# Attention by pairs of heads: two 64-column V products and four 32-column sums side by side in TensorE's array

## The chip, the cores and the metric

One core of one Trainium2 chip. The metric is the device time of one execution in microseconds (us). Engines: PE is TensorE, DVE is VectorE, ACT is ScalarE, POOL is GpSimd, and SP issues DMAs.

## The reference, cut to what matters

```python
def _attn_ref(q, k, v):                          # 4 batches, 8 heads, 576 positions, 64 wide
    scores = scale * np.matmul(q, k.transpose(0, 1, 3, 2))
    scores = np.where(block_i >= block_j, scores, -1e9)      # blocks of 64 positions
    scores = scores - np.max(scores, axis=-1, keepdims=True)
    attn = np.exp(scores)
    attn = attn / (np.sum(attn, axis=-1, keepdims=True) + 1e-09)
    return np.matmul(attn, v)

x = _moe_ref(x=attention_as_(2304, 512), ...)    # h = x @ w_in; (h * cos(h)) @ w_out
return _moe2_ref(x=x, ...)                       # 8 experts, weighted by a normalised gate
```

The change is in the attention alone, which stands first in the program.

## The kernel before

All on-chip tensors lie with the contracted index on partitions. `attention()` takes the 32 heads one after another, in an order written out by hand (the program order of each engine is the order of the calls). For head i the calls are:

- `load`, `high_both`, `high_parts`, `low_parts`, `move_k_lo`, `move_q_hi`: q and k of a later head are fetched and each split into a rounded high part and the rest (F32R operands `QA`, `KA`, `QB`, `KB`, two buffers each), by ACT, POOL, DVE and DMAs.
- `peak(i, 0)`, `peak(i, 1)`: six rough score products into PSUM tile `px`. `find` takes row maxima on DVE into `nm`, `turn` transposes them on PE, `maxima` puts them into rows of `QA` on DVE, so that the score product subtracts them.
- `weights(i, part)`, four parts: score products (12 F32R matmuls) into one-bank PSUM tiles `sp`, `sq`, `sr`, `sc`, each turned into weights by one exp on ACT (`ep`, `eq`, `er`, `ec`).
- `pv(i, c)`, c from 0 to 4: seven F32 matmuls with the weights as moving and a block of V as stationary operand into PSUM tile `o`. V of an even head has a 65th column of ones, V of an odd head is 128 wide (ones in column 0, V in 64 to 127), so that the sum of the weights comes out in one more partition of `o`.
- `evac(i)`: ACT copies `o` and the sums to SBUF. `sums`, `fetch`, `invert`, `give`, `spread` carry the sums of a pair of heads through DRAM, invert them and spread them over partitions; `scale` multiplies on DVE, `x_hi` and `x_lo` split the result into `xh`, `xl`.
- `some`, `conv.load`: steps of an unrelated conversion of weights, spread over the heads.

Behind the attention the feed-forward part begins with `h` products on the first rows of `xh`. An F32 matmul of the program appears in the trace as two instructions (x2), an F32R one as one.

Of the kernel before, what the change touches and what calls it, by code (L numbers as in the profile page):

```python
# [45 lines left out]
def attention_moe_kernel(ctx: ExitStack, tc: tile.TileContext, qk, v, w_a, gate, w_b, out):  # L46
# [11 lines left out]
    eps = top.tile([128, 80], F32, name="eps")[:, 0:2]  # L58
    nc.vector.memset(eps, 0.0)
    nc.vector.memset(eps[D:D + 1, 0:1], EPS)  # L60
    nc.vector.memset(eps[0:1, 1:2], EPS)
# [92 lines left out]
    def attention():  # L154
        with tc.tile_pool(name="at1", bufs=1) as p1, tc.tile_pool(name="at2", bufs=2) as p2, \
# [3 lines left out]
            KP = S + D  # L159

# [4 lines left out]
            KAP, KBP = (p1.tile([128, 2 * KP], F32R, name=n) for n in ("ka", "kb"))  # L165
            KA, KB = ([t[:, j * KP:j * KP + S] for j in range(2)] for t in (KAP, KBP))
            QB = [p1.tile([128, S], F32R, name=f"qb{j}") for j in range(2)]
            HI = p1.tile([128, S], F32R, name="hi")
# [8 lines left out]
            odd_sums = (post.tile([128, S], F32, tag="lt", name="rawl", bufs=1), tt[0])  # L177
# [5 lines left out]
            st, EP, EQ, ER, EC, SUMS, SR, INV, ps_t, ps_o = ({} for _ in range(10))  # L183
# [5 lines left out]
            def load(i):  # L189
                st[i] = p2.tile([128, S], F32, tag="st", name="st")  # L190
                nc.sync.dma_start(out=st[i][0:64, :], in_=qk[i][0:64, 1, :])
                nc.sync.dma_start(out=st[i][64:128, :], in_=qk[i][64:128, 0, :])

            def load_v(i):
                b, h = divmod(i, H)
                vt, c = V[i % 2], VC[i % 2]
# [18 lines left out]
            def pad():  # L215
                nc.gpsimd.memset(quarter, 0.25)
                ka, kb = (t.bitcast(F32).rearrange("p (j n) -> p j n", n=KP)[:, :, S:] for t in (KAP, KBP))
                nc.gpsimd.memset(kb, 0.0)
                nc.gpsimd.memset(ka[0:96], 0.0)
                nc.gpsimd.memset(ka[96:102], MASK)  # L220
                nc.gpsimd.memset(ka[96:101], -1.0)

            def zeros(j):
                nc.gpsimd.memset(QA[j][:, 0:64].bitcast(F32), 0.0)
                nc.gpsimd.memset(KA[j][64:128, :].bitcast(F32), 0.0)

            def minus(j):
                nc.gpsimd.memset(KA[j][96:101, :].bitcast(F32), -1.0)
                nc.gpsimd.memset(QA[j][96:102, 384:640].bitcast(F32), 1.0)
                nc.gpsimd.memset(NM[j], 0.0)  # L230

            def mask_q(j, copy):
                copy(QA[j][64:96, 64:640], diag[64:96, 64:640], None)

            def mask_k(j, copy):
                for h in range(2):
                    out = KA[j][64:72, 64:576].rearrange("p (t h n) -> p t h n", h=2, n=64)[:, :, h, :]
                    copy(out, step(1 - h), MASK)

            def by_dve(out, in_, factor):  # L240
                if factor is None:
                    nc.vector.tensor_copy(out=out, in_=in_)
                else:
                    nc.vector.tensor_scalar(out=out, in0=in_, scalar1=factor, scalar2=None, op0=ALU.mult)

            def by_act(out, in_, factor):
                nc.scalar.activation(out, in_, AF.Copy, scale=1.0 if factor is None else factor)
# [5 lines left out]
            def ones_of_v():  # L253
                nc.gpsimd.memset(V[0][:, :, D:D + 1], 1.0)
                nc.gpsimd.memset(V[1][:, :, 0:D], 0.0)
                nc.gpsimd.memset(V[1][:, :, 0:1], 1.0)

            def high_both(i):
# [1693 lines left out]
```

## Time and profile before

| | |
|---|---|
| median of 3 runs | 2051.07 us (2050.14 to 2052.83) |
| profiled execution, own time | 2051.26 us |
| its span in the trace | 2049.2 us |
| PE busy | 2038.3 us, 99% of the span |
| DVE, ACT, POOL busy | 77%, 52%, 36% |
| granted TensorE clock | 1.00, that is 2.4 GHz |
| attention on PE | from the start to 189.28 us |

Busy time of PE says that it always had a matmul in flight, not how full the array was. Starts of matmuls follow each other by the columns that they stream; their printed durations hold the way through the array too.

### The profile page before, as it was taken

The numbers are of one execution on the slowest core, as the hardware profiler recorded it, in microseconds if no ns is written. First come the engines' busy times: TensorE is split into PE (matmuls) and PEld (weight loads), VectorE is DVE, ScalarE is ACT, GpSimd is POOL, SyncE is SP. The second block draws the span as 40 slices with busy tenths as digits, with TensorE's granted clock in tenths as the row PEclk, the third lists the DMA queues.
The fourth block names the chain that finished last, engine by engine and source line by source line (L and its number), as shares of the span: only waits on it lengthen the run. The fifth ranks groups of instructions, "written<-read, shape, count | busy, mean of one in ns | idle before, by whom it ended". The sixth has DMA issues, their size and how long they took to land.

```text
span 2049.2 us, 34723 instructions
## 1 busy us (share of the span) xinstructions
PE 2038.3 (99%) x12549; PEld 1921.3 (94%) x12549; DVE 1577.4 (77%) x2801; ACT 1059.0 (52%) x1873; POOL 735.6 (36%) x569
## 2 busy tenths in 40 slices
PE   9999999999999999999999999999999999999999
PEld 7888999899989998989899999999999999999998
DVE  7887897876778788887776777777777777777776
ACT  7887775554464433334333444544455444445443
POOL 4553330000015444454541333344444333333332
PEclk9999999999999999999999999999999999999999
DMA  6666775574454577766666555555555655555552
GB/s 168 187 185 183 258 264 188 209 265 165 144 190 170 200 247 240 278 217 211 223 240 208 200 173 203 180 180 188 191 198 183 210 178 197 176 203 181 185 184 103
DMA packets 202714, 407.48 MB, mean 199 GB/s; under 512 B 44944, under 2 KB 90512, under 8 KB 202544
## 3 DMA queue, kind: packets, MB, share of 16 engines
q1 hardware_dynamic: 202544, 405.28, 58.6%
q8 instruction: 99, 1.62, 0.3%
q14 instruction: 71, 0.58, 0.1%
HBM read 289.48 MB, written 106.58 MB: 193 GB/s over the span
## 4 chain that ended last, share of the span: by engine, by line
PE 93%; DVE 3%; ACT 2%; DMA 1%; issue 0%; POOL 0%; ACTq 0%; SPq 0%; DVEq 0%
PE acc L846 8%; PE p L526 8%; PE p L525 7%; PE p L524 7%; PE hx L524 6%; PE hx L525 6%; PE hx L526 6%; PE acc L526 4%; PE acc L525 4%; PE acc L524 4%; PE o L360 4%; PE hy L525 3%; PE hy L524 3%; PE hy L526 3%; PE h L524 2%; PE h L526 2%
## 5 line engine op out<-in xcount | busy, mean ns | idle before, releaser
L1552 POOL TENSOR_TENSOR w<-s,w 128x512 fp32r<-128x512 f32 x148 | 232.8, 1573 | 403.1 <-ACT w L1551 382.4
L1648 DVE SCALAR_TENSOR_TENSOR oa<-p,P,oa 128x256 f32<-128x256 f32 x627 | 271.9, 477 | 69.3 <-PE p L526 67.5
L526 PE MATMUL p<-w,xl 128*128 128x256 f32 x870 | 245.1, 282 | 0.0
L525 PE MATMUL p<-w,xh 128*128 128x256 f32 x810 | 227.9, 281 | 0.0
L524 PE MATMUL p<-w,xh 128*128 128x256 f32 x810 | 227.4, 281 | 0.0
L666 POOL TENSOR_TENSOR wv<-stg,wv 128x512 fp32r<-128x512 f32 x62 | 110.9, 1807 | 226.9 <-ACT wv L662 215.3
L1552 POOL TENSOR_TENSOR w<-raw,w 128x512 fp32r<-128x512 f32 x73 | 115.1, 1577 | 186.2 <-ACT w L1551 180.4
L526 PEld LDWEIGHTS p<-w,xl 128*128 128x128 f32 x870 | 164.6, 189 | 0.1
L525 PEld LDWEIGHTS p<-w,xh 128*128 128x128 f32 x810 | 153.1, 189 | 0.0
L524 PEld LDWEIGHTS p<-w,xh 128*128 128x128 f32 x810 | 152.7, 189 | 0.0
L526 PE MATMUL acc<-wv,hs 128*128 128x512 f32 x384 | 150.8, 393 | 0.0
L525 PE MATMUL acc<-wv,hs 128*128 128x512 f32 x384 | 150.6, 392 | 0.0
L524 PE MATMUL acc<-wv,hs 128*128 128x512 f32 x384 | 150.0, 391 | 0.0
L629 POOL TENSOR_TENSOR s<-stg 128x256 f32<-128x256 f32 x60 | 47.2, 808 | 286.4 <-PE acc L846 282.3
L525 PE MATMUL p<-w,xl 128*128 128x256 f32 x492 | 138.2, 281 | 0.0
L524 PE MATMUL p<-w,xl 128*128 128x256 f32 x492 | 138.0, 280 | 0.0
L1493 DVE SCALAR_TENSOR_TENSOR oa<-acc,P,oa 128x512 f32<-128x512 f32 x168 | 123.8, 744 | 11.6 <-PE acc L526 10.8
L524 PE MATMUL hx<-th,w 128*128 128x384 f32 x384 | 129.4, 337 | 0.7 <-ACT c L1736 0.7
L525 PE MATMUL hx<-tl,w 128*128 128x384 f32 x384 | 128.8, 336 | 0.0
L526 PE MATMUL hx<-th,w 128*128 128x384 f32 x384 | 128.6, 335 | 0.0
L1590 ACT ACTIVATE xh<-raw 128x768 fp32r<-128x768 f32 x138 | 114.8, 840 | 14.5 <-DVE raw L1608 7.7
L526 PE MATMUL p<-w,xh 128*128 128x256 f32 x432 | 121.8, 282 | 0.6 <-DVE xh L1598 0.6
(388 smaller groups left out, 6351.3 us busy)
## 6 DMA issues: line engine op xcount, KB each, us to landing
w<-w1d SPq DMA_DIRECT2D x128, 512.0 KB
w<-w1d SPq DMA_DIRECT2D x128, 384.0 KB
stg<-in_w_b_dram SPq DMA_DIRECT2D x64, 512.0 KB
s<-td SPq DMA_DIRECT2D x83, 256.0 KB
s<-in_w_b_dram SPq DMA_DIRECT2D x65, 256.0 KB
wo<-wvd SPq DMA_DIRECT2D x32, 512.0 KB
w1d<-wah SPq DMA_DIRECT2D x32, 512.0 KB
w1d<-wal SPq DMA_DIRECT2D x32, 512.0 KB
```

The costliest lines, as they stand in the source:

```text
L360: nc.tensor.matmul(o[:, q0:q1], vt[:, c], e, start=c == 0, stop=True, skip_group_check=c > 0)
L524: nc.tensor.matmul(ps, lh, rh, start=first, stop=False, skip_group_check=go_on)
L525: nc.tensor.matmul(ps, lh, rl, start=False, stop=False, skip_group_check=go_on)
L526: nc.tensor.matmul(ps, ll, rh, start=False, stop=last, skip_group_check=go_on)
L629: eng.tensor_tensor(out=out, in0=in0, in1=in1, op=op)
L666: eng.tensor_tensor(out=t[:, DM:2 * DM], in0=src, in1=t[:, 0:DM].bitcast(F32), op=ALU.subtract)
L846: nc.tensor.matmul(acc[half, b][:, at:at + w_], w[:, s], h[:, t0:t0 + w_], start=f == 0 and i == 0 and at == 0, stop=f == F1 - 1 and i == ...
L1493: nc.vector.scalar_tensor_tensor(out=o, in0=acc, scalar=p, in1=o, op0=ALU.mult, op1=ALU.add)
L1552: nc.gpsimd.tensor_tensor(out=t[:, DM:2 * DM], in0=raw, in1=t[:, 0:DM].bitcast(F32), op=ALU.subtract)
L1590: nc.scalar.activation(self.h[o], self.get(o), func)
L1648: nc.vector.scalar_tensor_tensor(out=o, in0=ps, scalar=p, in1=o, op0=ALU.mult, op1=ALU.add)
```

## The change

Heads are taken in pairs p = (a, b). The V products of the two heads go into two halves of the array's columns (stationary operand 64 columns wide, output partitions 0 to 63 and 64 to 127 of the one PSUM tile `o`), alternating head by head. V has no column of ones; `pe_sums(p)` makes the sums by 20 matmuls of their own per pair with 32 columns of ones as stationary operand, in four column tiles (head h, column group t). `weights` has two parts with two-bank PSUM tiles `spq`, `src` and one exp each (832 and 768 columns). `evac` is two ACT instructions per pair. `QA`, `KA`, `QB`, `KB` have four buffers each. `scale` runs on POOL in the loop. `peak(.., "o")` and `turn(.., o)` use `o` as scratch between two pairs. The start brings four heads in before the first V products; `direct` splits q and k of heads 0 to 3 by ACT and POOL without DMAs.

```diff
-            V = [p1.tile([128, 336], F32, name="v0")[:, 0:5 * (D + 1)].rearrange("p (c n) -> p c n", n=D + 1), p1.tile([128, 5, 2 * D], F32, name="v1")]
-            VC = [slice(0, D), slice(D, 2 * D)]
+            V = [p1.tile([128, 5, 2 * D], F32, name=f"v{j}") for j in range(2)]
+            E = [[p1.tile([128, n], F32, name=f"e{n}") for n in (832, 768)],
+                 [far(n, F32, "e") for n in (832, 768)]]
...
+            o = pso.tile([128, 1024], F32, name="o")
...
+            def direct(i):
+
+                nc.scalar.activation(KB[i][64:128, 0:S], st[i][0:64, :], AF.Copy)
+                nc.scalar.activation(QB[i][0:64, :], st[i][64:128, :], AF.Copy)
+                for t, r in ((KB, slice(0, 64)), (QB, slice(64, 128))):
+                    nc.gpsimd.tensor_tensor(out=t[i][r, 0:S], in0=st[i][r, :], in1=HI[i % 2][r, :].bitcast(F32),
+                                            op=ALU.subtract)
...
+            def peak(i, u, tag):
...
+                ps = psx.tile([128, 1024], F32, tag="x", name="px") if tag == "x" else o
...
+            def turn(i, ps):
+                ps_t[i] = ps[0:101, 832:960]
+                nc.tensor.transpose(ps_t[i], NM[i % 2], ident)
...
-            def weights(i, part):
...
+            def weights(i, part, then=None):
+
+                at0, blocks = ((0, ((3, 320, 256, 256), (0, 256, 320, 0), (4, 320, 256, 576), (0, 0, 256, 512))),
+                               (64, ((1, 128, 448, 64), (2, 256, 320, 512))))[part]
+                ps = pst.tile([128, 1024], F32, tag=("pq", "rc")[part], name=("spq", "src")[part])
...
+                if then:
+                    then(ps)
+                e = E[i % 2][part]
+                nc.scalar.activation(e, ps[:, at0:at0 + (832, 768)[part]], AF.Exp, scale=0.125)
+                return ps
...
-            def pv(i, c):
-                m = D + 1 if i % 2 == 0 else 2 * D
...
+            def pv(p):
+                for c, q0, q1, part, at in ((0, 0, 256, 0, EQ), (0, 256, 576, 0, EP), (1, 128, 256, 1, ER),
+                                            (1, 256, 576, 1, ER + 128), (2, 256, 576, 1, EC),
+                                            (3, 384, 576, 0, EP + 320), (4, 512, 576, 0, EQ + 256)):
+                    for h in range(2):
+                        r = slice(h * D, (h + 1) * D)
+                        nc.tensor.matmul(o[r, 256 + q0:256 + q1], V[p % 2][:, c, r], E[h][part][:, at:at + q1 - q0],
+                                         start=c == 0, stop=True, skip_group_check=True)
+
+            def pe_sums(p):
+                for t, col, n, part, at, new in ((0, 0, 256, 0, EQ, True), (1, 832, 192, 0, EP + 128, True),
+                                                 (0, 832, 128, 0, EP, True), (1, 832, 192, 0, EP + 320, False),
+                                                 (0, 0 + 128, 128, 1, ER, False), (1, 960, 64, 0, EQ + 256, False),
+                                                 (0, 832, 128, 1, ER + 128, False), (1, 832, 192, 1, ER + 256, False),
+                                                 (0, 832, 128, 1, EC, False), (1, 832, 192, 1, EC + 128, False)):
+                    for h in range(2):
+                        r = slice(h * D + 32 * t, h * D + 32 * t + 32)
+                        nc.tensor.matmul(o[r, col:col + n], ones[:, 0:32], E[h][part][:, at:at + n],
+                                         start=new, stop=True, skip_group_check=True)
+
+            def evac(p):
+                nc.scalar.activation(RAW[p % 3], o[:, 256:832], AF.Copy)
+                nc.scalar.activation(sums_of[p % 2].rearrange("p (b n) -> p b n", n=256),
+                                     o.rearrange("p (b n) -> p b n", n=256)[:, 0::3], AF.Identity, bias=eps)
...
+            def scale(p, eng=nc.gpsimd):
+                eng.tensor_tensor(out=XF, in0=RAW[p % 3], in1=RB, op=ALU.mult)
...
+            edges(3)
+            direct(2)
+            high_both(3)
+            q_high(3)
+            k_high(3, KA)
+            px = peak(2, 0, "x")
...
+            sp = weights(1, 0)
...
+            sr = weights(1, 1)
+            direct(3)
+            px = peak(3, 0, "x")
+            turn(2, sp)
+            maxima(2)
+            find(*px)
+            pv(0)
...
+            pe_sums(0)
+            for p in range(1, NP):
...
+                    maxima(b)
...
+                evac(p - 1)
...
+                    if nxt:
+                        find(*peak(a1, 0, "x"))
+                    weights(a, 0)
+                    if nxt:
+                        f = peak(a1, 1, "o")
+                    weights(a, 1)
+                    if nxt:
+                        find(*f)
...
+                fetch(p - 1)
+                if nxt:
+                    f = peak(b1, 0, "x")
+                    weights(b, 0, lambda ps: turn(a1, o))
+                    find(*f)
+                    maxima(a1)
+                else:
+                    weights(b, 0)
+                sr = weights(b, 1)
+                if nxt:
+                    f = peak(b1, 1, "x")
+                pv(p)
+                if nxt:
+                    find(*f)
+                if p > 1:
...
+                    for i in (a2, b2):
+                        high_both(i)
+                        q_high(i)
+                        k_high(i, KA)
+                    for i in (a2, b2):
+                        low_parts(i)
+                        move_k_lo(i)
+                if p > 1:
+                    scale(p - 2)
+                invert(p - 1)
+                give(p - 1)
...
+                some(2 if p % 2 == 0 else 3)
...
+                pe_sums(p)
...
+                    turn(b1, sr)
```

PE, products of an even head with V before, from the middle of the attention (`o` is the output tile, `v_109` V with its ones, `px` and `pt` the rough scores and the transpose):

```order
L360 MATMUL o_1055<-ep_1034,v0_109 65x320
L360 MATMUL o_1055<-eq_1041,v0_109 65x256
L293 MATMUL px_1058<-ka_101,qa1_100 128x448
L293 MATMUL px_1058<-ka_101,qa1_100 128x320
L360 MATMUL o_1055<-er_1046,v0_109 65x128
L360 MATMUL o_1055<-er_1046,v0_109 65x320
L360 MATMUL o_1055<-ec_1051,v0_109 65x320
L320 MATMUL pt_1077<-ident_61,nm1_107 101x128
L360 MATMUL o_1055<-ep_1034,v0_109 65x192
L360 MATMUL o_1055<-eq_1041,v0_109 65x64
```

The same place after: the end of `pv` and the start of `pe_sums` of a pair (`e832`, `e768` are the weights of the first head, `e_122`, `e_123` those of the second):

```order
L357 MATMUL o_131<-e768_121,v1_119 64x320
L357 MATMUL o_131<-e_123,v1_119 64x320
L357 MATMUL o_131<-e832_120,v1_119 64x192
L357 MATMUL o_131<-e_122,v1_119 64x192
L357 MATMUL o_131<-e832_120,v1_119 64x64
L357 MATMUL o_131<-e_122,v1_119 64x64
L368 MATMUL o_131<-e832_120,ones_66 32x256
L368 MATMUL o_131<-e_122,ones_66 32x256
L368 MATMUL o_131<-e832_120,ones_66 32x192
L368 MATMUL o_131<-e_122,ones_66 32x192
```

The seven products of 65 or 128 output partitions per head have become fourteen of 64 per pair, and products of 32 output partitions with the tile of ones stand behind them; the rough scores no longer stand between them.

POOL, the start of the program before (the splits of head 0, then constants, then the first cast for head 1):

```order
L221 MEMSET ka_101 5x2x64
L254 MEMSET v0_109 128x5
L255 MEMSET v1_110 128x5x64
L256 MEMSET v1_110 128x5
L228 MEMSET ka_101 5x576
L229 MEMSET qa1_100 6x256
L230 MEMSET nm1_107 128x101
L263 CAST ka_101<-st_130 64x576
```

POOL, the start after, from the cast for head 2 to that for head 3:

```order
L268 CAST ka_107<-tla_127 64x576
L287 TENSOR_TENSOR kb1_102<-st_145,hi_114 64x576
L287 TENSOR_TENSOR qb1_104<-st_145,hi_114 64x576
L239 MEMSET qa_106 64x64
L240 MEMSET qa_106 6x256
L241 MEMSET ka_108 64x64
L242 MEMSET kb_110 128x64
L287 TENSOR_TENSOR kb_109<-tla_127,hi_113 64x576
L287 TENSOR_TENSOR qb_111<-tla_127,hi_113 64x576
L268 CAST ka_108<-tla_127 64x576
```

Four more subtractions (`TENSOR_TENSOR`, those of `direct(1)` and `direct(2)`) and four constants stand ahead of the cast `ka` for head 3, on which the first rough scores of head 3 wait; on PE these stand ahead of `pv(0)`.

## Rows read from the trace of the kernel before

**Rows 1.** The page: busy time, and the chain that ended last by engine.

```profile
PE 2038.3 (99%) x12549; PEld 1921.3 (94%) x12549; DVE 1577.4 (77%) x2801; ACT 1059.0 (52%) x1873; POOL 735.6 (36%) x569
...
PE 93%; DVE 3%; ACT 2%; DMA 1%; issue 0%; POOL 0%; ACTq 0%; SPq 0%; DVEq 0%
```

**Rows 2.** By stretch: us, then PE, PEld, DVE, ACT, POOL busy, clock, DMA share, GB/s.

```profile
100.12:111.30 11.18, 11.18 (x70) 9.28 (x68) 8.44 (x17) 9.28 (x17) 5.46 (x6) 1.00 0.69 192
16.00:189.28 173.28, 172.97 (x1017) 143.19 (x1017) 139.88 (x263) 141.08 (x260) 83.69 (x82) 1.00 0.65 175
```

**Rows 3.** Timeline of PE: start, us, engine, line, instruction; one pair of heads.

```profile
100.12 0.75 PE L293 MATMUL px<-ka,qa 68*128 68x256 f32 x4
100.71 0.28 PE L332 MATMUL sp<-qb,kb 128*128 128x256 f32 x1
...
102.45 0.70 PE L360 MATMUL o<-ep,v 128*65 128x320 f32 x2
102.99 0.59 PE L360 MATMUL o<-eq,v 128*65 128x256 f32 x2
...
104.54 0.70 PE L360 MATMUL o<-ec,v 128*65 128x320 f32 x2
105.08 0.34 PE L320 MATMUL pt<-ident,nm 128*101 128x128 f32 x1
105.25 0.49 PE L360 MATMUL o<-ep,v 128*65 128x192 f32 x2
...
111.30 0.75 PE L293 MATMUL px<-ka,qa 68*128 68x256 f32 x4
```

**Rows 4.** Groups by form, 16 to 190 us: weight loads of two widths (busy us, mean ns).

```profile
L360 PEld LDWEIGHTS o<-eq,v 128*128 128x128 f32 x64 | 11.7, 189 | 2.6
...
L360 PEld LDWEIGHTS o<-eq,v 128*65 128x65 f32 x60 | 8.2, 137 | 4.8
```

**Rows 5.** Timeline of PE around a gate product of 16 output partitions.

```profile
368.33 0.51 PE L846 MATMUL acc<-gh,wo 128*128 128x512 f32 x2
368.68 0.34 PE L559 MATMUL plt<-xh,ghl 128*16 128x384 f32 x1
...
369.90 0.34 PE L560 MATMUL plt<-xl,gz 128*16 128x384 f32 x1
370.07 0.51 PE L846 MATMUL acc<-gh,wo 128*128 128x256 f32 x2
```

**Rows 6.** Groups by form, 16 to 190 us: ACT and POOL (busy us, mean ns).

```profile
L404 POOL TENSOR_TENSOR xl<-tt,xh 128x576 fp32r<-128x576 f32 x13 | 18.3, 1406 | 6.1 <-ACT xh L400 6.1
L346 ACT ACTIVATE ep<-sp 128x512 f32<-128x512 f32 x31 | 18.1, 585 | 7.8 <-PE sp L333 7.8
...
L346 ACT ACTIVATE ec<-sc 128x320 f32<-128x320 f32 x31 | 13.1, 421 | 0.0
...
L369 ACT ACTIVATE tla<-o 64x576 f32<-64x576 f32 x16 | 10.3, 646 | 11.9 <-PE o L360 8.7 <-ACT hi L259 2.1 <-issue 1.1
...
L370 ACT ACTIVATE rawl<-o,eps 1x576 f32<-1x576 f32 x8 | 5.9, 733 | 0.1
```

**Rows 7.** Timeline of DVE in the same pair of heads.

```profile
101.50 1.15 DVE L315 TENSOR_REDUCE nm<-px 128x1 f32<-128x192 f32 x3
...
105.45 0.83 DVE L324 TENSOR_TENSOR qa<-pt,diag 5x640 fp32r<-5x640 f32 x1 [0.45 <-PE pt L320]
```

**Rows 8.** Timeline of POOL at the start of the program.

```profile
6.50 1.40 POOL L284 TENSOR_TENSOR qb<-st,hi 64x576 fp32r<-64x576 f32 x1
...
10.05 0.31 POOL L229 MEMSET qa<- 6x256 f32 x1
...
10.67 0.66 POOL L263 CAST ka<-st 64x576 fp32r<-64x576 f32 x1
```

**Rows 9.** Timeline of PE at the end of the attention.

```profile
184.84 0.39 PE L333 MATMUL sp<-qa,ka 101*128 101x256 f32 x1 [0.31 <-DVE qa L324]
...
189.28 0.42 PE L524 MATMUL h<-xh 128*128 128x384 f32 x1
```

More of the change, by code (lines that the diff above doesn't have):

```diff
@@ L57, in attention_moe_kernel @@
     nc.vector.memset(half_pi, float(np.pi / 2))
[L58 to L61, printed above, removed]
+    eps = top.tile([128, 80], F32, name="eps")[:, 0:1]
+    nc.vector.memset(eps, EPS)
     xh = top.tile([128, NC, N], F32R, name="xh")
@@ L215, in pad @@
             def pad():
[L216 to L225, printed above, removed]
@@ L240, in by_dve @@
[L240 to L247, printed above, removed]
+                nc.gpsimd.memset(KB[0][:, S:].bitcast(F32), 0.0)
+                nc.gpsimd.memset(KA[0][0:96, S:].bitcast(F32), 0.0)
@@ new lines, in edges, with constants @@
+            def edges(j):
+                nc.gpsimd.memset(QA[j][0:64, 0:64].bitcast(F32), 0.0)
+                nc.gpsimd.memset(QA[j][96:102, 384:640].bitcast(F32), 1.0)
+                nc.gpsimd.memset(KA[j][0:64, S:].bitcast(F32), 0.0)
+                nc.gpsimd.memset(KB[j][:, S:].bitcast(F32), 0.0)
+            def constants(j):
+                for t, r in ((KA, slice(64, 102)), (QA, slice(64, 96))):
+                    nc.sync.dma_start(out=t[j][r, :].bitcast(F32), in_=t[0][r, :].bitcast(F32))
@@ L249, in tiles, with mask_q, mask_k @@
+            def mask_q():
+                nc.vector.tensor_copy(out=QA[0][64:96, 64:640], in_=diag[64:96, 64:640])
+            def mask_k():
+                for h in range(2):
+                    out = KA[0][64:72, 64:576].rearrange("p (t h n) -> p t h n", h=2, n=64)[:, :, h, :]
+                    nc.scalar.activation(out, step(1 - h), AF.Copy, scale=MASK)
             def tiles():
@@ L509, in attention @@
-            evac(NH - 1)
-            sums(NH - 1)
-            e = NH - 2
-            n = 4
-            more = [(tla[:, 0:DM], odd_sums[0][:, 0:DM]), (tt[0][:, 0:DM], RAW[1][:, 0:DM])]
-            return conv, [[t.bitcast(I32) for t in pair] for pair in more], {0: lambda: spread(e - 2), n: lambda: (x_hi(e - 4), x_lo(e - 4)), n + 1: lambda: scale(e - 2),
-                              n + 2: lambda: (x_hi(e - 2), fetch(e)),
-                              n + 3: lambda: (x_lo(e - 2), invert(e), give(e)), n + 4: lambda: spread(e),
-                              n + 6: lambda: scale(e), n + 7: lambda: x_hi(e), n + 8: lambda: x_lo(e)}
+            q_high(1)
@@ new lines, in attention @@
+            high_both(1)
+            k_high(1, KA)
+            nc.gpsimd.memset(NM[1], 0.0)
+            edges(2)
+            high_both(2)
+            k_high(2, KA)
+            direct(1)
+            load(4)
+            load(5)
+            q_high(2)
+            turn(0, idle)
+            maxima(0)
+            px = peak(1, 0, "x")
+            find(*px)
+            weights(0, 0)
+            px = peak(1, 1, "o")
+            find(*px)
+            weights(0, 1)
+            edges(3)
+            direct(2)
@@ new lines, in attention @@
+            evac(NP - 1)
+            sums(NP - 1)
+            p = NP - 1
+            n = 4
+            more = [(tla[:, 0:DM], sums_of[0]), (tt[0][:, 0:DM], RAW[1][:, 0:DM])]
+            return conv, [[t.bitcast(I32) for t in pair] for pair in more], {0: lambda: spread(p - 1), n: lambda: (x_hi(p - 2), x_lo(p - 2)), n + 1: lambda: scale(p - 1, nc.vector),
+                              n + 2: lambda: (x_hi(p - 1), fetch(p)),
+                              n + 3: lambda: (x_lo(p - 1), invert(p), give(p)), n + 4: lambda: spread(p),
+                              n + 6: lambda: scale(p, nc.vector), n + 7: lambda: x_hi(p), n + 8: lambda: x_lo(p)}
```

335 lines of the change are left out of this document (145 added, 190 removed).

## Prediction

> **What bounds the kernel now.** I read the page first, then the busy time by stretch, then PE's timeline inside one pair of heads. On the page PE is busy for 99% of the span and makes 93% of the chain that ended last [rows 1]. That says only that PE never waits, so the question is whether it also never waits in the attention. It does not: in the pair of heads from 100.12 to 111.30 us PE is busy for all 11.18 us, and from 16 us to the end of the attention for 172.97 of 173.28, at full clock; ACT is the next one with 9.28 of 11.18, DVE has 8.44, POOL 5.46 [rows 2]. The attention ends on PE at 189.28 us, where the first `h` product starts, and behind it PE stays bound [rows 1, 9]. So the attention is worth its PE time, and each microsecond won or lost in it comes through to the end as long as another engine does not become the limit.
>
> What a matmul costs is read from the distance of starts, not from the printed duration. An F32 V product of 320 columns stands as two passes: 102.45 to 102.99 is 0.54 us, and 104.54 to 105.08 again [rows 3]. That is 0.27 us a pass or 0.84 ns a column and pass.
>
> **What goes.** The seven V products of a head stream 320, 256, 128, 320, 320, 192 and 64 columns, 1600 together. With two passes at 0.84 ns that is 2.70 us a head, 5.40 of the 11.18 us of a pair. The column of ones cost nothing before, since it widened only the stationary side. The other 5.78 us (24 score products, 12 rough scores, two transposes and the small gaps between them) stay on PE in the same number and shapes.
>
> **What comes: V products.** The same slices are streamed for both heads, 2 x 1600 columns, into different halves of the array. If the halves run at the same time the pair costs 2.70 us, if one after another 5.40. The trace of before has no two matmuls side by side, so these are the bounds. I take 2.70: each half has its own output partitions, its own weights and its own moving data.
>
> **What comes: sums.** 20 matmuls per pair, 1600 columns for each head, split over two column groups of 768 and 832 columns. One after another they would cost 5.40 us. Four streams that run freely cost what the longest does, 832 x 2 x 0.84 = 1.40 us. Streams that move in rounds of four (two heads, two groups) cost the longest of each round: 256, 192, 128, 192 and 192 columns, together 960, times 2 x 0.84 ns = 1.61 us. Weight loads could pace them instead: 189 ns for 128 columns and 137 ns for 65 [rows 4] is 0.83 ns a column, so 27 ns for 32; 40 loads (two a matmul) make 1.1 us, less than the streams. I take 1.60, since the calls stand in such rounds, with 1.40 and 5.40 as ends.
>
> **Waits that the change adds on PE.** `o` is now scratch for rough scores and for a transpose, and single. (1) `peak(a1, 1)` waits for `evac(p - 1)`. By ACT's rows the two copies cost 646 ns and, for 512 columns with a bias, 733 - 64 x 0.85 = 679 [rows 6], 1.33 us; PE has the transpose (0.17 us, 105.08 to 105.25), four rough scores (0.59, 100.12 to 100.71) and eight score products to do meanwhile; all twelve of a head stream 3712 columns in the 1.74 us to 102.45, 0.47 ns each, so these eight with 2176 take 1.02 [rows 3]. Cost nothing, and 0.3 if ACT comes late to it. (2) The V products wait for `maxima(a1)` on DVE, which reads the transpose out of `o`: three maxima 1.15 and `maxima` 0.83 [rows 7], 1.98 us behind the rough scores of b1; PE's work between is 1.02 + 0.17 + 0.72 (1536 columns) + 0.36 (768 columns) = 2.27 us. (3) They wait for the second head's exp: the slope from 421 ns at 320 columns to 585 at 512 [rows 6] is 0.85 ns a column, so 0.86 us for 832; PE has the 0.72 + 0.36 us of other work. Both are close, and what queues behind them is all of PE. I put 0.3 us a pair on (1) to (3) together, with 0 and 0.8 as bounds.
>
> **Engines that hide the rest.** On the same slope the four exps of a head (512, 320, 448 and 320 columns) are 1.96 us and the two new ones 1.66, so ACT loses 0.6 us a pair; `evac` had three instructions of 0.65 to 0.73 [rows 6] and has 1.33 us now, 0.8 less. From 9.28 ACT falls to about 7.9. DVE loses `scale`. POOL takes it: at the price of the neighbouring 128x576 operation, 1.41 us [rows 6], POOL rises from 5.46 to about 6.9. The moved DMAs (three fetches for one, sums of four partitions) sit on SP's queue ahead of loads that are needed one pair later, over 10 us away. All this is free while a pair lasts 10 us.
>
> **Start and end.** Pair 0 cannot begin its V products before `peak(3, 0)`, which waits on POOL. As in the trace, head 0's second subtraction ends at 6.50 + 1.40 = 7.9 us [rows 8]. Behind it stand three casts of 0.66, four subtractions of 1.41 and nine constants of 0.1 to 0.31 [rows 8], 9.4 us with small gaps: 17.3 to 17.5 us. Then 0.6 us of rough scores and a transpose: the V products of pair 0 start at about 18.1 us, and PE has idled for some 2 to 3 us before. Pair 0 ends at 18.1 + 2.70 + 1.60 = 22.4 us. The last pair lacks rough scores and a transpose (1.4 us less), but has no work to cover its exps and copies (1.5 us more, my estimate from the exps above; before, the last head idles 0.31 us [rows 9]).
>
> **The sum.** A pair costs 11.18 - 5.40 + 2.70 + 1.60 + 0.3 = 10.38 us. Fifteen follow pair 0: 22.4 + 155.7 + 0.1 = 178.2 us against 189.28, 11.1 us sooner. The profiled execution takes 2051.26 us, 2.1 more than its span, and the median of the runs is 2051.07; so I forecast 2051.1 - 11.1 = 2040 us. With freely running sums and no waits a pair costs 9.88 and the attention ends at 170.5: 2032.
>
> **Rivals.** *The passes lock step (slower).* Each F32 matmul is two passes on the same tile [rows 3], and the second can't start before the first is through. If PE starts matmuls strictly in order, that second pass holds up the first pass of the next tile, however many tiles there are: only neighbours overlap, and every matmul costs one pass length. V products still cost 3200 x 0.84 = 2.70, but the sums 2.70 too. A pair costs 11.48, the attention ends at 23.5 + 172.2 + 0.1 = 195.8 us, 6.5 later: 2057.6. It decides from the point where the sums exceed about 2.3 us. Against it: two passes on one tile are all that the trace of before has, so nothing there shows it either way. The Trainium skill, "TensorE: Matmul & The Clock Gate", section "Part 3: Packing small matmuls", says that matmuls start and end in program order without reordering, while those on different tiles overlap; it gives 2.38 times for three column tiles, of single-pass matmuls as far as the page tells, and no run here shows it.
>
> *Changing the tiling costs a drain.* A pair changes the array's division three times (whole, halves, quarters, whole). If the array must empty each time, the price is the way through the array: a 384-column product lasts 0.34 us while starts follow at 0.17 [rows 5], so 0.17 a change, 0.5 us a pair. On top of the forecast: 22.9 + 163.2 + 0.1 = 186.2, 2048. The row against it: the gate products, which have 16 output partitions, come 0.35 us behind the two passes ahead of them and the next work 0.17 behind the last, the same distances as without a change [rows 5]. "TensorEngine Tiling (Array Packing)" in the Trainium skill, section "Key Properties", states that a change of mode drains the engine. The rows on the gate products do not agree with it, though they need not be a changed mode for the hardware.
>
> *No overlap at all.* V products 5.40 and sums 5.40 a pair: 16.9 us, the attention ends at about 282, 2144 us. It needs F32 passes to claim the whole array; nothing in the trace excludes it.
>
> *Another engine takes over.* At 10.4 us a pair ACT's 7.9 is too little to bound; only the chains (2) and (3) could. With 0.8 instead of 0.3 a pair the time is 2048.
>
> **Chances.** Side by side in rounds, as forecast: 0.52 (its own range 2031 to 2047). With a drain or with the waits at their upper bound: 0.16 (2044 to 2052). Lock step: 0.22 (2055 to 2064, the upper end with a drain). No overlap: 0.07. The remainder, a longer start above all, 0.03. The range from 2030 to 2060 leaves out no overlap and the worst of lock step. What a measurement of this kernel can tell from no change is 0.2%, 4 us: faster means below 2047. Of the first case 0.51 is faster and 0.01 the same; of the second 0.06 faster, 0.08 the same and 0.02 slower; of lock step 0.03 the same and 0.19 slower; the rest is slower. That makes 0.57, 0.12 and 0.31.
>
> **What would show it.** Right: starts of V products of the two heads nearly together or overlapping, 2.7 us from the first to the first sum; sums of 1.4 to 1.7 us; pairs 10.4 us apart; `h` starting near 178 us. Lock step shows as sums of 2.7 us. A drain shows as gaps ahead of the first V product, the first sum and the transpose behind. The start is right if PE idles on POOL's cast for head 3 until about 17.5 us. The forecast falls if `o` or its readers hold PE longer than the 0.3 us, or if the two halves do not overlap.

## The result, and the profile after

The changed kernel takes **2063.07 us** (median of 4 runs, 2061.62 to 2065.4), the kernel before 2051.62 in the same series: 1.0057 times as long, with an interval of 1.004 to 1.0075. Slower by 11.5 us, where 2040 was forecast. The profiled execution has a span of 2061.1 us.

First the busy time by stretch (columns as in [rows 2]): a pair of heads in the middle, from sums to sums; an early pair; the attention; what follows it.

```profile
103.66:116.04 12.38, 10.52 (x109) 8.76 (x106) 9.34 (x18) 8.44 (x13) 7.19 (x8) 1.00 0.68 180
16.00:202.94 186.94, 169.78 (x1658) 139.17 (x1656) 133.12 (x244) 128.19 (x183) 97.09 (x97) 0.95 0.61 163
46.04:56.27 10.23, 10.23 (x109) 8.70 (x107) 9.28 (x17) 8.51 (x13) 5.26 (x6) 1.00 0.70 180
202.94:2061.00 1858.06, 1851.96 (x11469) 1767.90 (x11467) 1425.97 (x2514) 906.84 (x1594) 641.83 (x460) 1.00 0.59 201
```

The attention ends at 202.94 us, 13.7 later than before [rows 9]; the remainder takes what it took (1858.1 against 2049.2 - 189.28 = 1859.9). PE, which never waited [rows 2], idles 17 of 187 us, and nobody else is full: DVE 9.34 of 12.38, ACT 8.44, POOL 7.19. Yet the early pair takes 10.23 us, all of it PE's. So PE's work has shrunk nearly as forecast, and something makes PE wait later on.

PE's timeline: the sums of each pair start where L368 stands, then one pair from its V products to the wait.

```profile
18.61 2.92 PE L357 MATMUL o<-e,v 128*64 128x256 f32 x28
21.46 1.62 PE L368 MATMUL o<-e,ones 128*32 128x256 f32 x40
35.86 1.62 PE L368 MATMUL o<-e,ones 128*32 128x256 f32 x40
46.04 1.62 PE L368 MATMUL o<-e,ones 128*32 128x256 f32 x40
56.27 1.62 PE L368 MATMUL o<-e,ones 128*32 128x256 f32 x40
68.31 1.62 PE L368 MATMUL o<-e,ones 128*32 128x256 f32 x40
...
100.77 2.96 PE L357 MATMUL o<-e,v 128*64 128x256 f32 x28
103.66 1.62 PE L368 MATMUL o<-e,ones 128*32 128x256 f32 x40
105.21 0.35 PE L324 MATMUL src<-ident,nm 128*101 128x128 f32 x1
105.32 0.74 PE L303 MATMUL px<-ka,qa 68*128 68x256 f32 x4
...
106.94 0.51 PE L303 MATMUL o<-ka,qa 68*128 68x448 f32 x2
108.99 0.47 PE L335 MATMUL src<-qb,kb 128*128 128x448 f32 x1 [1.54 <-DVE qa L327]
...
201.39 1.62 PE L368 MATMUL o<-e,ones 128*32 128x256 f32 x40
```

V products take 2.89 us a pair (100.77 to 103.66), sums 1.55. The last instruction ahead of each change of the array's division (whole, halves, quarters, whole) is

```profile
100.53 0.31 PE L303 MATMUL px<-ka,qa 68*128 68x320 f32 x1
103.51 0.22 PE L357 MATMUL o<-e,v 128*64 128x64 f32 x1
104.95 0.33 PE L368 MATMUL o<-e,ones 128*32 128x192 f32 x2
```

and what follows starts 0.24, 0.15 and 0.26 us later. In the kernel before, the same step from 320 score columns to V products is 0.14 us (102.31 to 102.45), and a pass of 64 or 192 columns is worth 0.05 or 0.16 at 0.84 ns a column:

```profile
102.31 0.30 PE L333 MATMUL sc<-qa,ka 101*128 101x320 f32 x1
```

So each of the three changes costs about 0.1 us that no column accounts for, 0.3 us a pair. The second and the third distance are the same in every pair of the changed kernel.

The steps from sums to sums are 14.40 in the second pair, then 10.18, 10.23, and from there 12.04 and the like; the fifteen together are 201.39 - 21.46 = 179.9, 12.00 on average. At 108.99 PE stands 1.54 us for `maxima(b)`. DVE's timeline says why that is late:

```profile
103.41 0.95 DVE L274 TENSOR_TENSOR qb<-st,hi 128x576 fp32r<-128x576 f32 x1 [0.18 <-DMA tt<-inv]
106.82 0.25 DVE L387 RECIPROCAL sc<-sc 72x16 f32<-72x16 f32 x1 [2.46 <-DMA sc<-sums]
...
108.11 0.83 DVE L327 TENSOR_TENSOR qa<-src,diag 5x640 fp32r<-5x640 f32 x1
```

The reciprocal, a quarter of a microsecond, stands 2.46 us at the head of DVE for the sums to come back from DRAM, and the maxima stand behind it. Between 60 and 180 us DVE waits so for 16.2 us in all; before it was 1.0. And SP's queue, which the prediction had called free, issues DMAs almost without a gap in this pair:

```profile
98.73 1.10 SPq L208 DMA_DIRECT2D v<-in_v_dram  x2
99.92 0.56 SPq L378 DMA_DIRECT2D sums<-rawl  x1
100.58 1.12 SPq L396 DMA_DIRECT2D tt<-inv  x2
101.76 1.23 SPq L280 DMA_DIRECT2D qb<-qa  x2
103.08 2.26 SPq L383 DMA_DIRECT2D sc<-sums  x3
105.39 0.83 SPq L90 DMA_DIRECT2D cw<-in_w_a_dram  x2
106.33 1.10 SPq L277 DMA_DIRECT2D kb<-qb  x2
107.61 0.43 SPq L391 DMA_DIRECT2D inv<-sc  x1
108.13 0.49 SPq L199 DMA_DIRECT2D st<-in_qk_dram  x1
108.68 0.59 SPq L200 DMA_DIRECT2D st<-in_qk_dram  x1
109.36 0.55 SPq L199 DMA_DIRECT2D st<-in_qk_dram  x1
109.96 0.59 SPq L200 DMA_DIRECT2D st<-in_qk_dram  x1
110.64 1.11 SPq L208 DMA_DIRECT2D v<-in_v_dram  x2
```

19 issues from 98.73 to 110.64 us: 11.91 us, of which only the fetch of the sums (2.26; 1.24 where it has not to wait, in the kernel with three issues less, below) is stretched. Bare that is about 10.9 us a pair, already more than the 10.38 forecast.

The trace of before held the warning: in it 18 issues follow each other from 98.58 to 109.40 us, 10.82 us of a pair's 11.18. Between 60 and 180 us both kernels issue 190 DMAs, one every 0.63 us, though PE is full in one and waits in the other. 19 at that distance make 12.0 us, which is the average step.

### The profile page after: what moved, and what is told of

The parts are those of the page before. It is cut to its first block, busy times and chain, and to the rows that moved or that the text cites. A ratio compares the mean times of both kernels' runs of the same rounds, so it can differ in the third digit from the quotient of the medians.

```text
span 2061.1 us, 35874 instructions
## 1 busy us (share of the span) xinstructions
PE 2033.7 (99%) x13189; PEld 1917.9 (93%) x13189; DVE 1569.9 (76%) x2783; ACT 1047.6 (51%) x1796; POOL 753.2 (37%) x591
## 4 chain that ended last, share of the span: by engine, by line
PE 89%; DVE 4%; ACT 2%; SPq 1%; POOL 1%; issue 1%; DMA 1%; DVEq 0%; ACTq 0%; POOLq 0%
PE acc L916 8%; PE p L596 7%; PE p L595 7%; PE p L594 7%; PE hx L594 6%; PE hx L595 6%; PE hx L596 6%; PE acc L596 5%; PE acc L595 5%; PE acc L594 5%; PE hy L595 3%; PE hy L594 3%; PE hy L596 3%; PE h L594 2%; PE h L596 2%; PE h L595 2%
## 5 line engine op out<-in xcount | busy, mean ns | idle before, releaser
L1563 DVE SCALAR_TENSOR_TENSOR oa<-acc,P,oa 128x512 f32<-128x512 f32 x168 | 123.8, 744 | 11.5 <-PE acc L596 10.6
```

Of the source, the lines that this page charges most:

```text
L1563: nc.vector.scalar_tensor_tensor(out=o, in0=acc, scalar=p, in1=o, op0=ALU.mult, op1=ALU.add)
```

## The experiments

**The reciprocal first.** The obvious culprit is DVE's wait. Theory one: only the place of `invert` is wrong. Its rival then: the single PSUM tiles and DVE's own work set the pair; the queue was not yet suspected. *Reciprocal later*: `invert` and `give` of a pair are called one pair later, the moves of q ahead of them.

```diff
-                if p > 1:
-                    spread(p - 2)
...
+                if p > 1:
+                    invert(p - 2)
+                    give(p - 2)
+                    spread(p - 2)
...
-                invert(p - 1)
-                give(p - 1)
```

> The reciprocal of pair p - 1 and the DMA behind it are called one pair later, behind the row maxima of the next pair, where the sums have long landed; the moves of q and k stand ahead of it on SP. Theory (DVE, which works in order, stands at the reciprocal for the DMA with the sums, and the maxima that free the `src` tile stand behind it): the waits of PE on the maxima (L327, 1.2 to 1.6 us in most pairs) go below 0.3 us, the stretches of low clock go too, a pair takes 10.2 to 10.6 us, `h` starts at 178 to 182 us and the time is 2038 to 2043 us. Rival (the single PSUM tiles `o` and `src` and DVE's own amount of work set the pair, the reciprocal is only what stands there): PE waits about as long on another maximum or exp, and the time stays above 2055.

Measured: 2078.08 us (1.0123, interval 1.0106 to 1.014). The wait moved. In the waits of that kernel, 46 to 200 us, SP's queue now stands for the reciprocals to land, the loads behind it come late for ACT, POOL waits for the spread and PE for DVE:

```profile
POOL tt L403 <- DMA tt<-inv: 69.1, 11, 7.3
...
ACT hi L261 <- DMA st<-in_qk_dram: 19.5, 16, 2.2
...
PE px L303 <- DVE nm L319: 10.8, 14, 2.5
...
SPq L396 <- DMA inv<-sc: 22.1, 12, 3.2
```

Theory one falls. *No wait for the sums*: the reciprocal takes a constant tile, so the output is scaled by a constant and not by the sums; the DMAs stay.

```diff
-                nc.vector.reciprocal(out=SC, in_=SC)
+                nc.vector.reciprocal(out=RD, in_=RC)
```

> Everything stands as in the changed kernel, but the reciprocal reads and writes small tiles that no DMA touches (a constant 576), and that result is spread, so the output is scaled by a constant instead of the sums; the sums still travel, and nobody reads them. Theory of the wait on the sums' DMA: as good as calling it later, 2037 to 2043 us. Rival that the place and the work on DVE count, not the DMA: no change from 2063.

Measured: 2058.61 us (1.0035, 1.0023 to 1.0047): 4.5 us back of the 23 to the forecast, between the theory's 2037 to 2043 and the rival's 2063. DVE's wait is gone. PE now stands ahead of the first score products (3.10 us at 105.60), which read what the queue's moves bring; the profile names no releaser there.

**What the tiles do.** Both on top of the later reciprocal, one run each. *Heads in turn* puts all V products of one head ahead of the other's:

```diff
-                for c, q0, q1, part, at in (...
-                    for h in range(2):
+                for h in range(2):
+                    for c, q0, q1, part, at in (...
```

> On top of the reciprocal called later: the fourteen V products of a pair stand head by head instead of alternating. If matmuls start in program order and overlap only with neighbours on other tiles, the V products of a pair take about 5.4 us instead of 2.87, and the time is some 40 us above that of the alternating version, 2075 to 2085. If the array's queue reaches past seven matmuls, they stay at 2.9 us and the time does not move.

*Two tiles* streams the sums of the first column group of both heads, then those of the second:

```diff
+                for g in range(2):
                     for t, col, n, part, at, new in blocks:
                         for h in range(2):
+                            if t != g:
+                                continue
```

> On top of the reciprocal called later: the sums of the first column group of both heads stand ahead of those of the second, so that two of the four 32-column tiles alternate at a time. If all four run side by side only when they stand in turns, the sums take about 1600 x 2 x 0.84 ns = 2.7 us instead of 1.55, some 18 us in all, 2056 to 2062. If the order of the calls does not matter, 1.55 us and no change.

Measured 2081.3 and 2076.89 us, against 2078.08. PE's timeline, two rows of the heads in turn, then one of two tiles:

```profile
97.10 5.24 PE L357 MATMUL o<-e,v 128*64 128x256 f32 x28
102.27 1.62 PE L368 MATMUL o<-e,ones 128*32 128x256 f32 x40
```

```profile
97.90 2.51 PE L372 MATMUL o<-e,ones 128*32 128x256 f32 x40
```

V products one head after the other take 5.17 us, side by side 2.89: a full factor of 1.8 that needs neighbours on different tiles. The sums take 2.5 us by two tiles and 1.6 by four. And 2.3 us more of PE a pair cost 3 us in all, not 40: in the kernel with the later reciprocal PE is not the limit. That 2081 lies in the range that was expected is luck, since that range stood on 2040 for the heads side by side. With the heads in turn eight of the fifteen steps are 12.29 to 12.30 us, which is PE's own pace there.

**The queue.** The second theory: what paces a pair is the number of issues on SP's queue. One kernel with fewer issues and the same bytes, one with more, one with still fewer, and the kernel before with fewer as a control. *Three issues less*: the host lays k and q, and the V of two heads, side by side, so one DMA brings each.

```diff
-                nc.sync.dma_start(out=st[i][0:64, :], in_=qk[i][0:64, 1, :])
-                nc.sync.dma_start(out=st[i][64:128, :], in_=qk[i][64:128, 0, :])
+                nc.sync.dma_start(out=st[i], in_=qk[i])
...
+                if i % 2:
+                    return
+                vt, rows = V[i // 2 % 2], v.rearrange("p s d -> (p s) d")
```

> Theory now: what paces a pair of heads in the changed kernel is SP's queue, which carries 19 DMA issues a pair one after another, 11.4 us from start to start without the wait in front of the fetch of the sums, and stands without a gap over the 12.4 us of a pair. Here the two halves of q and k of a head come in one issue and the V of both heads in one, so 16 issues, and about 3 x 0.58 = 1.75 us less. A pair then takes 10.6 to 11.0 us, the waits of the reciprocal and of the matmuls on q and k shrink, and the time is 2037 to 2045 us. Rival: the chain of exps, maxima and rough scores through two single PSUM tiles paces the pair; then the number of issues does not matter and the time stays at 2058 to 2063. A miss of another kind: a merged issue lasts as long as the two that it replaces; then SP's queue is as full as before and the time stays too, but the queue's rows show it.

*Two issues more*, ahead of `scale`:

```diff
+                for _ in range(2):
+                    nc.sync.dma_start(out=dr.tile([64, 128], F32, tag="z", name="z"), in_=ident[0:64, :])
```

> The changed kernel with two more DMAs a pair on SP's queue, each of 64 rows of 512 bytes that nobody reads. If SP's queue paces the pair: 2 x 0.5 to 0.55 us more in each of 15 pairs, so 2078 to 2080 us. If the PSUM chain paces it: within 3 us of 2063.

*Four issues less* has one more merged:

```diff
-                    for n in range(2):
-                        conv.load(p // 2 + 1, None, p % 2 * 2 + n)
+                    conv.load(p // 2 + 1, None, p % 2)
```

> The kernel with three issues less, and the two pieces of the w_a weights of a pair in one issue, so 15 a pair. If SP's queue paces the pair until PE does: another 0.4 us a pair less until PE's own 10.3 us are reached, so 2034 to 2041 us and 0 to 6 us below the kernel with three issues less. If the PSUM chain paces it: 2058 to 2063.

*Before, merged* is the kernel before with the one DMA for k and q:

> The kernel before with q and k of a head in one issue (two issues a pair less). In it PE is busy for all of a pair's 11.18 us and SP's queue waits for engines in some 20 of 120 us, so if each kernel is paced by the engine that the theory names, nothing is gained: within 2 us of 2051. If merged loads help whatever is the bound (by data that land earlier, say), it gains as the changed kernel does, 10 us or more.

Measured: three less 2049.9 us (0.9997 of before, 0.9988 to 1.0006), 13.2 below the changed kernel; two more 2075.35, 12.3 above it (2078 to 2080 expected); four less 2050.4, no more than three, where up to 6 were expected; before, merged 2049.95 (0.9998, 0.9988 to 1.0007), no gain. The rival, the chain through the PSUM tiles, said 2058 to 2063 for three less and is out. The queue with three less has gaps again, and in `kb` it stands for DVE, though the same data move:

```profile
100.34 1.24 SPq L381 DMA_DIRECT2D sc<-sums  x3
101.62 0.82 SPq L90 DMA_DIRECT2D cw<-in_w_a_dram  x2
102.56 1.99 SPq L275 DMA_DIRECT2D kb<-qb  x2
105.14 0.33 SPq L389 DMA_DIRECT2D inv<-sc  x1
105.55 0.81 SPq L199 DMA_DIRECT2D st<-in_qk_dram  x2
106.42 0.43 SPq L207 DMA_DIRECT2D v<-in_v_dram  x1
```

A merged load of 128 rows is issued in 0.4 us, less than either half took. The issues were the price, not the bytes; the transfers run faster in the last kernel below (210 GB/s against 180). One thing is not separated: the merged V also has rows of 512 bytes in DRAM in place of 256, and the control merges only q and k. The time of three less lands 5 to 13 us above what was expected, so the queue is not all.

**Does PE count again, and how near was the kernel before?** *Heads in turn, fewer issues* is the order of above on the kernel with three less:

> The kernel with three issues less, with all V products of one head ahead of those of the other. With the full queue this order cost nothing (2081 against 2078 us) though the V products of a pair took 5.17 us in place of 2.86. If PE paces the pair once the queue is shorter, the 2.3 us show: 15 x 1.9 to 2.3 us more than 2049.9, so 2078 to 2085 us. If another engine still paces it, under 2060.

*Before, two more* adds one DMA a head to the kernel before:

```diff
+                    nc.sync.dma_start(out=dr.tile([64, 128], F32, tag="z", name="z"), in_=ident[0:64, :])
```

> The kernel before with one more DMA a head (two a pair) on SP's queue, of the same size as in the dose on the changed kernel, where two a pair cost 12 us. Before, the queue has 18 issues, about 10.2 us bare of a pair's 11.18, so there is about 1 us of room. If PE paces that kernel and the queue has that room: 0 to 4 us more, 2051 to 2055. If the queue paced it already: 15 x 1.1 us, 2066 or more.

Measured: 2074.47 us, 24.6 more than with the heads side by side (3.5 to 10.5 under what was expected), where the full queue had hidden it. Every step but that of the second pair and the last is 12.29 or 12.30 us, PE alone. And 2061.09 us for before with two more (1.0053, 1.004 to 1.0066): 10.3 us, a miss. So the kernel before had almost no room either, though PE was busy throughout: its queue had 18 issues, and the two cost it nearly what they cost the changed kernel. This is the cleanest of the doses: PE is busy for 110.36 of the 120 us from 60 to 180, before for all 120, and the granted clock is 1.00 in both. In that time it issues 194 DMAs, the changed kernel with two more 193, against 190 without: more issues a pair hardly raise the number of issues in a given time, they make the pairs longer. With three less it is 175, and the queue has gaps.

**What is missing to 2040.** On the kernel with three less. *Reciprocal later, fewer issues* is the first experiment again with room on the queue, two tiles for the sums and the spread behind the fetch; *start* also asks for head 3's high parts ahead of head 2's split.

```diff
                         find(*peak(a1, 0, "x"))
+                    invert(p - 2)
...
+                if p > 1:
+                    give(p - 2)
...
+                fetch(p - 1)
+                if p > 1:
+                    spread(p - 2)
                 if nxt2:
```

> The kernel with three issues less still takes 10.5 to 11.9 us a pair: DVE stands before the reciprocal for the sums (1.97 us at 104.86), maxima(b) behind it comes late, and PE stands 1.10 us for it. Here the reciprocal of a pair is asked for one pair later behind find(a1, 0), the fetch of the sums and the spread of the reciprocals stand behind the w_a loads on SP's queue, and the sums have two tiles. If SP's queue has room now, as the theory says (16 issues, about 9.7 us of 10.4), this takes the wait off DVE and a pair falls to 10.3 to 10.5 us: 15 x 0.5 = 7 us less than 2049.9, so 2040 to 2045 us. If the queue is still the limit, the new wait of the spread for the reciprocals makes it slower, as in the first experiment: 2055 or more.

```diff
             edges(3)
+            q_high(3)
+            k_high(3, KA)
             direct(2)
             high_both(3)
-            q_high(3)
-            k_high(3, KA)
```

> The kernel with three issues less and the later reciprocal, and at the start the two copies of the high parts of head 3 stand ahead of the split of head 2, on which PE waits 0.98 us on POOL there. 0 to 2 us below the kernel without it, if POOL is the limit of the start; no difference if the other copies that now come later are.

Measured 2050.92 and 2049.7 us, neither of the outcomes expected of the first; the 1.2 us between them lie within the spread of their runs. The wait is no harm now, and no help. *Copies behind the exps* moves what waits for POOL out of ACT's way, and *order, all issues* is the same with 19 issues:

```diff
-                if p > 2:
-                    x_hi(p - 3)
-                    x_lo(p - 3)
...
                 sr = weights(b, 1)
+                if p > 2:
+                    x_hi(p - 3)
+                    x_lo(p - 3)
```

> With 16 issues a pair, the later reciprocal and the shorter start, pairs still take 10.0 to 11.4 us (the second 16.2), and PE waits ahead of the V products for the exps (0.94 us at 96.23): on ACT the copy x_hi of an older pair stands ahead of the exps of the second head and waits 1.1 to 2.5 us for POOL's scale. Here x_hi and x_lo stand behind those exps, the copies of both heads that DVE waits for come ahead of the two casts of q, and one piece of the w_a work stands ahead of them in odd pairs. If this is what holds the pair: 0.5 to 0.8 us less in each of 12 pairs, so 2040 to 2045 us from 2049.7. If the pair is held by the DMA chain of the sums or by SP's queue still: 2048 to 2051.

> The same order of the engines' work, but q, k and V loaded in the 19 issues a pair of the changed kernel. If SP's queue has no room for 19 issues in a pair of 10.4 us (11.4 us bare), this gives a pair of 11.5 to 12.3 us, 2055 to 2066 us, whatever order the engines have. If the order was what held the changed kernel and not the number of issues: within 4 us of the kernel beside it.

Measured 2049.63 (0.999, 0.9981 to 0.9999), against the theory's 2040 to 2045, and 2056.12 us (1.0026, 1.0017 to 1.0035), as the queue's theory said. With the order alike, three issues are worth 6.5 us; the order is worth 7 to the changed kernel and nothing to the shorter queue: PE now waits for POOL's casts behind `x_lo` (3.8 us in four waits between 46 and 200 us). *Spread last* and *fetch behind moves* take the waits for landings from in front of the loads:

```diff
-                if p > 1:
-                    spread(p - 2)
...
                     load(b2 + 2)
+                if p > 1:
+                    spread(p - 2)
```

The second has, on top of that:

```diff
-                fetch(p - 1)
                 if nxt2:
...
                         move_k_lo(i)
+                fetch(p - 1)
```

> With the exps freed, PE waits for POOL's casts of k (1.21 us at 113.75, 1.52 at 136.90), behind them ACT's copies for the loads of q and k: the loads stand on SP's queue behind the spread, which waits until the reciprocals have landed, and POOL's scale in front of the next casts waits for the spread. Here the spread stands last of a pair on SP's queue, the scale a pair later, and x_lo behind the casts. Theory: with no wait for a landing ahead of the loads, the queue (16 issues, 9.7 us bare) is no limit and PE sets the pair, 10.0 to 10.4 us: 2038 to 2044 us. Rival: the queue holds a pair above 10.7 us wherever the waits stand, or the second pair and the start cost what is missing: 2047 to 2050.

> The same, and the fetch, which waits for the sums to land, stands behind the moves of the low parts of k on SP's queue, with the reciprocal one maximum later on DVE. If the wait of the fetch still holds the queue in the kernel beside it: 2 to 5 us less than that one. If not: within 2 us of it.

Measured 2073.16 and 2085.53 us, both against the theory. In the waits of the first POOL stands for the spread and everything behind POOL's scale follows:

```profile
POOL tt L404 <- DMA tt<-inv: 68.5, 12, 8.3
ACT xh L407 <- POOL tt L404: 20.5, 10, 3.3
DVE qb L275 <- ACT hi L262: 19.1, 6, 4.1
```

*Subtraction behind casts* leaves the spread where it was and puts `x_lo` behind the casts of k; *give first* puts the write of the reciprocals ahead of the moves of q:

```diff
                     x_hi(p - 3)
-                    x_lo(p - 3)
...
+                if p > 2:
+                    x_lo(p - 3)
                 if p > 1:
                     scale(p - 2)
```

```diff
+                if p > 1:
+                    give(p - 2)
                 if nxt:
                     for i in (a1, b1):
                         move_q_hi(i)
                         k_high(i, KB)
-                if p > 1:
-                    give(p - 2)
```

> The kernel with x_hi behind the exps, and on POOL x_lo behind the casts of k instead of ahead of them, with the spread where it was (moving it to the end cost 23 us). In that kernel PE waits for POOL's casts 0.85 to 1.5 us in four of ten pairs. If the order on POOL is what is left: 2042 to 2047 us. If not, 2048 to 2051.

> The same, and the write of the reciprocals ahead of the moves of q on SP's queue, so that they land 1.1 us earlier and the spread waits less. If the spread's wait holds the loads: 1 to 4 us less than the kernel beside it. If the moves of q become late, or the write waits for the reciprocal in front of them: as much more.

Measured 2047.54 us (0.9983, 0.9974 to 0.9992) and **2044.54 us** (0.9972, 0.9963 to 0.9981), 18.5 below the changed kernel and 6.1 below the one before. The 3 us between these two are not clear of noise: their intervals overlap. One pair of the last, by stretch:

```profile
57.81:67.79 9.98, 9.98 (x110) 8.30 (x106) 9.00 (x17) 8.22 (x13) 6.67 (x8) 1.00 0.76 210
```

Nine of the last kernel's fifteen steps are 9.98 to 10.1 us, PE alone. Its attention ends at 184.42 us.

## Why the prediction was wrong

**What PE has to do was nearly right.** V products 2.89 us a pair for 2.70, sums 1.55 for 1.60. A pair in which PE is never idle takes 10.23 in the changed kernel, 9.98 at best in the last one, for 10.08 without the 0.3 of waits. The lock step (sums of 2.70) and the missing overlap (16.9 a pair) did not come. The order of calls in rounds of four, on which the 1.60 rested, does matter: 2.5 us without it.

That the sum of PE's terms came out so well is in part luck. The cost of a change of tiling, a rival that the forecast put at nothing, did come: about 0.1 us a change in place of the rival's 0.17, 0.3 a pair in place of 0.5. The one behind the V products is half of what they took beyond 2.70. The Trainium skill ("TensorEngine Tiling (Array Packing)", section "Key Properties") says that a change of mode drains the engine, and these rows agree; whether the time is a drain or a weight load that can't run ahead was not separated. On the other side, the score products, rough scores and transposes took 5.58 us in the last kernel (9.98 - 2.85 - 1.55) for 5.78. The weight loads of 32 columns were read wrong: 27 ns is the slope alone, while the two rows of [rows 4] leave some 80 ns at no columns, and the trace has 105 to 111 ns. The 40 of a pair, 4.4 us one after another, must have overlapped, since the sums take 1.55.

**The start was nearly right.** V products of pair 0 at 18.61 for 18.1, behind POOL's cast as said; pair 0 ends at 23.0 for 22.4.

**The step that failed** is the sentence that the moved DMAs, three fetches for one, "sit on SP's queue ahead of loads that are needed one pair later" and that this is "free while a pair lasts 10 us", and with it the 0.3 us (0.8 at most) of waits. I costed each engine's busy time and not the queue's. Three fetches of some 0.4 us each in place of one, and one issue less of sums, make 19 issues; 10.9 us bare do not fit in 10.38, and the 18 of before (10.82 in the pair named above, of which `v` was stretched by 0.4) would just have filled it. The queue falls behind after the lead that the start gives is used up (10.18, 10.23, then 12.04), the sums come back late, DVE stands for them, and PE behind DVE: 1.8 us a pair on average over what PE needs. The doses show it from both sides: two issues more +12.3 us, three less -13.2; in the kernel before, the same two +10.3 and two less nothing. The doses on the changed kernel hold some of the clock too: from 60 to 180 us it was 0.89 with two more, 0.97 in the changed kernel and 1.00 with three less. The dose on the kernel before does not. That the transfers themselves were the limit is spoken against by the merged loads, which move the same bytes.

The sum closes. Against the forecast's end at 178.2 us: start 0.6, the second pair, which runs in its own order, 14.40 - 10.38 = 4.0, and the other fourteen 165.5 - 145.3 = 20.2, together 24.8 of the measured 24.7. The second pair is an error of its own, the same in the last kernel (14.41). There it is 4.0 of the 6.2 us by which the attention ends after the forecast; the start (2.6) and one step of 13.81 are the rest and more, since most steps are shorter than 10.38.

**The rivals.** "Another engine takes over" was the right kind, at 0.5 us a pair above the forecast where it cost 1.4, and looked for on ACT, DVE and POOL. A rival of the right sign stood there with another mechanism: lock step at 2057.6, which would have decided on PE, where the trace shows nothing of it.

**The clock.** In the changed kernel the granted clock falls to the lower of its two levels (1.2 and 2.4 GHz) three times, from 29.8 to 33.2, from 135.6 to 142.4 and from 183.4 to 190.2 us. Ahead of these PE had stood for 1.21, 2.73 and 1.44 us; after 1.58 us at 83.4 and 1.55 at 107.5 the clock did not fall.

```profile
56.27:127.88 71.61, 63.66 (x640) 52.47 (x637) 53.80 (x100) 50.58 (x73) 40.05 (x40) 1.00 0.66 176
135.60:142.40 6.80, 6.73 (x27) 5.57 (x29) 4.30 (x9) 4.17 (x6) 5.28 (x6) 0.50 0.67 181
```

The long steps of 16.56 and 15.21 us hold the two later ones, and the second pair the first. The clock is not the cause of the loss: the six pairs from 56.27 to 127.88 take 11.94 us each at a granted clock of 1.00. What it adds was not measured by itself. An upper bound, estimated from the rows, is half of 3.4 + 6.8 + 6.8 us, 8.5 us of PE's work.

**What stays open:** why the later orders respond as they do (spread last +23 us) beyond the waits shown; that the doses come through at 0.7 to 0.9 us a pair for some 1.1 to 1.75 of issues; and whether the second pair can be put in the order of the others. That loads issued from another engine's queue would do as well was not tried.

## What to carry to other kernels

Before a loop is made shorter, add up the issues of its DMA queue as if it were an engine: their number times the distance from start to start, plus each place where the queue stands for a transfer to land. A queue that just fits in the old loop with 18 issues is the limit of a shorter one with 19, and the busy times of the page do not show it, since issues are not counted as busy; the queue's own timeline does. An engine that is busy for 100% of the time tells nothing of how near the next limit is: a small dose of extra work on each queue does.

## What the runs showed of the hardware

An issue occupies the queue for 0.33 to 0.6 us, and one of 128 rows no longer than one of 64 (0.4 against 0.5 to 0.6). "DMA: Bandwidth & Descriptors" in the Trainium skill, section "Issuing engines are not separate DMA queues", calls the time to start a DMA usually small beside the DMA itself; with a pair's 19 it was the limit here. F32 matmuls, two passes each, run side by side in halves (1.8 times) and quarters of the array, if neighbours in program order lie on different tiles: 5.17 us became 2.89. A change between the whole array, halves and quarters cost about 0.1 us each.
